# Soft-capped attention and two expert layers on one core: first loads in another order, fewer warming products, the first weight conversion at another place

## The chip, the cores and the metric

The kernel runs on one core of one Trainium2 chip. The time is the device time of one execution in microseconds; the median of three runs is given, and one more execution was taken by the hardware profiler.

## The reference

Three stages run in a row. The attention has 2 batches, 12 heads, 448 tokens and 64 columns a head; its scores are capped by a tanh. Two feed-forward layers follow on the 896 tokens with 768 columns. All is in 32-bit floats, except that the weights w_in, w_out of both layers come as 64-bit floats and are converted on the chip.

```python
scores = cap * np.tanh((q @ k.T / sqrt(64)) / cap)
attn = exp(scores - max(scores)); attn = attn / (sum(attn) + 1e-09)
x = (attn @ v)                                  # heads side by side: 896 x 768
h = x @ w_in                                    # 768 x 2048
x = (s * max(h, 0) ** 2 + b) @ w_out            # 2048 x 768
h = x @ w2_in                                   # 768 x 1024
so = h * softmax(h); ln = (so - mean) / sqrt(var + 1e-06) * g_ln
out = ln @ w2_out                               # 1024 x 768
```

## The kernel before, in words

**The start.** All that the first two pairs of heads need is loaded ahead of a branch. The keys go through load_by_key (line 98, its DMA is L104 when it is called by pair), the queries through load_by_query (line 119, its DMA is L123) or directly (L140). A DMA is issued by the engine whose queue is named: nc.sync is SyncE (SP in the profile), nc.scalar ScalarE (ACT), nc.gpsimd GpSimd (POOL). Each engine issues in its program's order. The scalar cap comes by L144; VectorE makes its absolute value a_t (L171), its reciprocal and the score factor sc_t from it, and each engine loads a_t (L183) and branches on it (L1006): up to 32 the arm layers(arm, False) runs, which is the case here (cap is 30). Meanwhile TensorE multiplies a tile of ones by itself 24 times (L170; in the profile each 32-bit product is two records), which gives no result that is used: the warming products.

**The attention.** The 24 heads are worked on as 12 pairs (0 to 11), four heads (two pairs) to a load group (0 to 5). For a pair, prep (line 401) turns keys and queries by products with an identity matrix (tiles pk, pq, L413), and splits each into a high and a low part: ScalarE makes the queries' high part (qh, L424), VectorE the rest. scores_by_key (line 441) makes four score tiles c = 0 to 3 of three product terms each on TensorE (s, L451), and ScalarE takes the tanh of each into e (L456). exps_by_key (line 459) has two exponentials on ScalarE (L463), two additions over the key blocks on GpSimd (c, L468 and L469) and two VectorE steps (L472). products_by_key (line 479) multiplies by the values (o, L484), and values_by_key (line 491) sums the rows by a product with ones (m, L498), and divides.

The loop over n runs from 0 to 13: it takes the scores of pair n, the exponentials of pair n - 1, the products of pair n - 2 and the prep of pair n + 2. on_pe keeps TensorE's instructions in the written order; tc.issue_after(x) queues the instructions of its block that run on x's engine behind x, and has no effect on other engines. The rest is placed by a scheduler. The next groups are loaded by load_group (line 379) when n is odd.

**The conversion.** The class Weights loads 64-bit weights into two buffers (raws, those that held the first keys and queries), 768 KB at a time from SyncE's queue (L281), and converts a block in steps: the first is an absolute value on ScalarE (L224), then VectorE steps (L225, L229, L234, L238), and a last step on both (L244, L245). weights.pump(1) takes one step in every turn of the loop from n = 3 on. It stands in `with tc.issue_after(st["dve"].ins)`, st["dve"] being VectorE's last instruction of values_by_key. weights.load(1) issues the loads of the first two blocks at n = 1.

**Behind the attention** both layers run as long rows of products on TensorE with the conversions beside them.

Of the kernel before, what the change touches and what calls it, by code (L numbers as in the profile page):

```python
# [37 lines left out]
def tile_softcap_attention__relu2__solu(  # L38
# [15 lines left out]
    nc = tc.nc  # L54
# [4 lines left out]
    P = 128  # L59
# [28 lines left out]
    cap_t = cst.tile([P, 1], F32, name="cap_t")  # L88
# [30 lines left out]
    def load_by_query(t, src, b, heads, eng=None):  # L119

        for pr in range((heads.stop - heads.start) // 2):
            for j in range(2):
                (eng or nc.sync).dma_start(  # L123
                    out=t[:, pr, :, j],
                    in_=src[b, heads.start + 2 * pr + j].rearrange("(p c) d -> p c d", c=NC),
                )

    first = {}
    for raw, nm, rows in ((raws[0], "k", P), (raws[1], "q", CP)):
        first[nm] = raw.bitcast(F32)[:rows, :4 * NC * D].rearrange(  # L130
            "p (n c h d) -> p n c h d", n=2, c=NC, h=2
        )
    for pr in range(2):
        pair = slice(2 * pr, 2 * pr + 2)
        odd = nc.scalar if pr == 0 else nc.sync
        for _ in load_by_key(first["k"][:, pr:pr + 1], k, 0, pair, by_pair=True, odd=odd):
            pass
        if pr == 0:
            for j, queue in enumerate((nc.sync, nc.scalar)):
                queue.dma_start(  # L140
                    out=first["q"][:, 0, :, j],
                    in_=q[0, j].rearrange("(p c) d -> p c d", c=NC),
                )
            nc.scalar.dma_start(out=cap_t, in_=cap.partition_broadcast(P))  # L144
        else:
            load_by_query(first["q"][:, 1:], q, 0, pair)
    ident = cst.tile([P, P], F32, name="ident")
    make_identity(nc, ident)
    s_t = cst.tile([P, 1], F32, name="s_t")
# [16 lines left out]

    with psum("ps_w", 1) as ps_w:
        idle = ps_w.tile([P, 512], F32, name="idle")
        for n in range(24):
            nc.tensor.matmul(idle[:D, :D], lhsT=ones, rhs=ones, start=True, stop=True)  # L170
    nc.vector.tensor_scalar(  # L171
        out=a_t.bitcast(U32), in0=cap_t.bitcast(U32), scalar1=0x7FFFFFFF, scalar2=None,
# [4 lines left out]
        out=sc_t, in0=r_t, scalar1=1.0 / float(D) ** 0.5, scalar2=None, op0=ALU.mult  # L177
# [7 lines left out]
    def layers(ctx, general):  # L185
# [191 lines left out]
        def load_group(g, names=("k", "q", "v")):  # L377
            b, i = divmod(g, GB)
            heads = slice(4 * i, 4 * i + 4)
            for nm, src in (("k", k), ("q", q), ("v", v)):  # L380
                if nm not in names:
                    continue
                by_key = nm != "q" and not general
                if g == 0 and (nm == "q" or nm == "k" and by_key):
                    nat[nm, g] = first[nm]
                    continue
                by_pair = nm != "v"
                shape = [P, 2, NC, 2, D] if by_pair else [P, 4, NC * D]
                t = ap_.tile(shape, F32, tag=f"{nm}n", name=f"{nm}n{g}", bufs=3)
                if by_key:  # L390
                    for _ in load_by_key(t, src, b, heads, by_pair):
                        pass
                elif by_pair:
                    t = t[:CP]
                    load_by_query(t, src, b, heads)
                else:
                    t = t[:CP]
                    nc.sync.dma_start(out=t, in_=by_query(src, b, heads))
                nat[nm, g] = t

        split = {}
        st = {}
# [41 lines left out]
        def scores_by_key(n, c):  # L444
            if c == 0:
                st["e", n] = ap_.tile([P, 7, S], F32, tag="e", name=f"e{n}", bufs=3)
            ps = ps_s.tile([P, 2, 512], F32, tag="s", name=f"s{n}_{c}")
            both = (slice(0, D), slice(D, P)) if c < 3 else (slice(0, P),)
            for x, (kk, qq) in enumerate(terms(n)):
                for j, rows in enumerate(both):  # L450
                    st["pe"] = nc.tensor.matmul(  # L451
                        ps[:, j, :S], lhsT=kk[rows, c * P:(c + 1) * P], rhs=qq[rows],
                        start=(x == 0), stop=(x == 2),
                    )
            m = len(both)
            nc.scalar.activation(  # L456
                out=st["e", n][:, 2 * c:2 * c + m, :], in_=ps[:, :m, :S], func=AF.Tanh
            )

# [214 lines left out]
        load_group(0, ("v",))  # L674
        load_group(2, ("k", "q"))
        load_group(1, ("v",))
        load_group(2, ("v",))
        NPR = NH // 2
        preps = {}

        def prep_half(n):
            if n < NPR:
                if n not in preps:
                    preps[n] = prep(n)
                next(preps[n], 0)

        if general:
            for n in range(NPR + 2):
                for c in range(NC):
                    i, c2 = 2 * n + c // 2, c % 2  # L690
                    if i < NH:
                        scores(i, c2)
                    if 0 <= i - 1 < NH:
                        exps(i - 1, c2)
                    if 0 <= i - 2 < NH:
                        transposes(i - 2, 2 * c2)
                        transposes(i - 2, 2 * c2 + 1)
                    if c < 2:
                        prep_half(n + 1)
                if n % 2 == 1 and n // 2 + 3 < NG:  # L700
                    load_group(n // 2 + 3)
                if n >= 2:
                    values(n - 2)
        else:
            def on_pe(step, *args):

                with tc.issue_after(st["pe"].ins):
                    step(*args)

            prep_half(1)  # L710
            prep_half(1)
            for n in range(NPR + 2):
                now, last = n < NPR, n >= 2
                for c in range(NC):
                    if now:
                        on_pe(scores_by_key, n, c)
                    if c == 1:
                        if 0 <= n - 1 < NPR:
                            exps_by_key(n - 1)
                        if last:  # L720
                            on_pe(products_by_key, n - 2, 0)
                if last:
                    on_pe(products_by_key, n - 2, 1)
                on_pe(prep_half, n + 2)
                on_pe(prep_half, n + 2)
                if last:
                    on_pe(values_by_key, n - 2)
                    with tc.issue_after(st["dve"].ins):
                        weights.pump((n > 2) if now else 3)
                if n == 1:  # L730
                    weights.load(1)
                if n % 2 == 1 and n // 2 + 3 < NG:
                    load_group(n // 2 + 3)
        att.close()
# [310 lines left out]
```

## Time and profile before

| | before |
|---|---|
| median of three runs | 484.4 us (482.73, 484.40, 484.58) |
| span of the profiled execution | 481.5 us; the page gives no other time of it |
| TensorE (PE) busy | 463.8 us, 96% |
| VectorE (DVE) busy | 352.2 us, 73% |
| ScalarE (ACT) busy | 275.8 us, 57% |
| GpSimd (POOL) busy | 88.6 us, 18% |
| mean granted TensorE clock | 0.989 |
| mean DMA rate | 102 GB/s |

The span runs from the first to the last instruction, and a run's time holds a little more. Busy time counts the instructions that work, not those that issue DMAs, branch or wait. A granted clock of 1.00 is 2.4 GHz, 0.50 is 1.2 GHz.

### The profile page before, as it was taken

Reading aid. Unit: us, or ns where it says so; the run is one execution under the profiler, and the core shown is the slowest. Engines: PE = TensorE matmul, PEld = TensorE weight load, DVE = VectorE, ACT = ScalarE, POOL = GpSimd, SP = SyncE. Lnnn points to the kernel's source line nnn. Section 1 sums busy time; section 2 is a strip of 40 time slices with the busy share of each in tenths; the row PEclk is TensorE's granted clock in tenths of the full one; section 3 lists DMA queues with packets and bytes.
Section 4 is the critical chain, followed back from the end, with each engine's and each line's share of the span. In section 5 each row is a group of like instructions: output and inputs, shape, how many; then the busy total and the mean of one; then the engine's idle time right before and its main releaser. Section 6 shows DMA issues by size and latency. Waiting matters only on the chain.

```text
span 481.5 us, 6595 instructions
## 1 busy us (share of the span) xinstructions
PE 463.8 (96%) x2432; PEld 376.6 (78%) x2432; DVE 352.2 (73%) x566; ACT 275.8 (57%) x398; POOL 88.6 (18%) x93
## 2 busy tenths in 40 slices
PE   7696999999999999999999999999999999999995
PEld 6443444444889989889988889989888898999894
DVE  3354999999898999996599988998958984043110
ACT  2877889982486577675577855555535552133120
POOL 4463879797000000000000000000001010000000
PEclk9898999999999999999999999999999999999998
DMA  4567533000456676642123324344312300011112
GB/s 96 126 177 170 121 96 103 1 1 0 154 175 195 210 230 207 181 159 83 50 87 89 93 88 139 124 136 165 131 66 67 131 1 13 21 33 34 34 45 61
DMA packets 47577, 49.28 MB, mean 102 GB/s; under 512 B 24496, under 2 KB 39984, under 8 KB 47536
## 3 DMA queue, kind: packets, MB, share of 16 engines
q1 hardware_dynamic: 46352, 48.54, 34.3%
q8 instruction: 21, 0.34, 0.3%
q10 hardware_dynamic: 1088, 0.23, 0.2%
q14 instruction: 20, 0.16, 0.1%
q0 software_dynamic: 96, 0.01, 0.0%
HBM read 46.01 MB, written 2.75 MB: 101 GB/s over the span
## 4 chain that ended last, share of the span: by engine, by line
PE 90%; SPq 5%; issue 2%; DMA 1%; ACTq 0%; ACT 0%; DVE 0%; DVEq 0%
PE in L329 8%; PE in L328 8%; PE y L330 8%; PE y L329 8%; PE y L328 8%; PE in L330 8%; PE o L484 7%; PE s L451 6%; PE h L919 4%; PE h L915 4%; PE h L923 4%; PE o L966 4%; PE o L965 4%; PE o L964 4%; SPq L104 2%; PE m L498 2%
## 5 line engine op out<-in xcount | busy, mean ns | idle before, releaser
L329 PE MATMUL in<-xl,h_wi 128*128 128x510 f32 (+2 forms) x192 | 70.0, 365 | 0.0
L328 PE MATMUL in<-xh,h_wi 128*128 128x510 f32 (+2 forms) x192 | 69.8, 365 | 0.0
L330 PE MATMUL in<-xh,l_wi 128*128 128x510 f32 (+2 forms) x192 | 69.6, 364 | 0.0
L900 POOL TENSOR_SCALAR va<-vs 128x1 f32<-128x1 f32 x7 | 2.0, 288 | 321.3 <-ACT e L899 321.3
L360 ACT ACTIVATE gh<-g,s_t 128x510 fp32r<-128x510 f32 (+1 forms) x64 | 42.2, 668 | 18.8 <-PE y L330 18.6
L361 DVE SCALAR_TENSOR_TENSOR gl<-g,s_t,gh 128x510 fp32r<-128x510 f32 (+1 forms) x64 | 42.7, 681 | 2.9 <-ACT gh L360 2.8
L484 PE MATMUL o<-e,vn 128*64 128x448 f32 x192 | 41.8, 561 | 0.0
L463 ACT ACTIVATE e<-e,a_t 128x1792 f32<-128x1792 f32 (+1 forms) x24 | 40.7, 1696 | 0.7
L456 ACT ACTIVATE e<-s 128x896 f32<-128x896 f32 (+1 forms) x48 | 36.6, 816 | 6.1 <-PE s L451 4.0
L329 PEld LDWEIGHTS in<-xl,h_wi 128*128 128x128 f32 x192 | 36.0, 188 | 5.0 <-issue 1.4
L328 PEld LDWEIGHTS in<-xh,h_wi 128*128 128x128 f32 x192 | 36.0, 188 | 4.3 <-issue 0.7
L330 PEld LDWEIGHTS in<-xh,l_wi 128*128 128x128 f32 x192 | 36.0, 188 | 3.6
L964 PE MATMUL o<-w2o_h,lh 128*128 128x384 f32 (+1 forms) x104 | 35.6, 342 | 0.5 <-ACT lh L206 0.5
L966 PE MATMUL o<-w2o_h,ll 128*128 128x384 f32 (+1 forms) x104 | 35.4, 342 | 0.0
L965 PE MATMUL o<-w2o_l,lh 128*128 128x384 f32 (+1 forms) x104 | 35.4, 340 | 0.0
L915 PE MATMUL h<-w2i_h,yh 128*128 128x512 f32 x84 | 33.0, 393 | 0.0
L919 PE MATMUL h<-w2i_l,yh 128*128 128x512 f32 x84 | 33.0, 392 | 0.0
L923 PE MATMUL h<-w2i_h,yl 128*128 128x512 f32 x84 | 32.8, 390 | 0.0
L472 DVE SCALAR_TENSOR_TENSOR c<-c,e 64x448 f32<-64x448 f32 x24 | 26.4, 1100 | 8.1 <-POOL c L469 7.7
L224 ACT ACTIVATE wt_wi<-raw 128x768 f32<-128x768 f32 x16 | 14.6, 911 | 27.7 <-DMA raw<-in_moe_w_in_dram 16.8
L451 PEld LDWEIGHTS s<-qh,kh 64*128 64x128 f32 (+1 forms) x84 | 9.3, 191 | 25.4 <-ACT e L456 17.4
L468 POOL TENSOR_TENSOR c<-e 128x896 f32<-128x896 f32 x12 | 25.3, 2111 | 20.0 <-ACT e L463 10.5
(422 smaller groups left out, 1110.1 us busy)
## 6 DMA issues: line engine op xcount, KB each, us to landing
raw<-in_moe_w_in_dram SPq DMA_DIRECT2D x16, 768.0 KB, 4.9
raw<-in_moe_w_out_dram SPq DMA_DIRECT2D x24, 512.0 KB, 3.6
raw_w2i<-in_moe_w_in_dram SPq DMA_DIRECT2D x12, 512.0 KB, 4.4
raw<-in_moe_w_out_dram SPq DMA_DIRECT2D x8, 768.0 KB, 4.4
qn<-in_q_dram SPq DMA_DIRECT2D x20, 112.0 KB, 3.0
vn<-in_v_dram SPq DMA_DIRECT2D x12, 128.0 KB, 3.2
kn<-in_k_dram SPq DMA_DIRECT2D x20, 64.0 KB, 2.5
vn<-in_v_dram SPq DMA_DIRECT2D x12, 96.0 KB, 3.0
```

The costliest lines, as they stand in the source:

```text
L328: nc.tensor.matmul(o, lhsT=wh, rhs=xh, start=first, stop=False)
L329: nc.tensor.matmul(o, lhsT=wh, rhs=xl, start=False, stop=False)
L330: nc.tensor.matmul(o, lhsT=wl, rhs=xh, start=False, stop=last)
L360: nc.scalar.mul(out=gh[:, :m], in_=r2, mul=s_t)
L361: nc.vector.scalar_tensor_tensor(out=gl[:, :m], in0=r2, scalar=s_t, in1=full(gh[:, :m]), op0=ALU.mult, op1=ALU.subtract,)
L484: st["pe"] = nc.tensor.matmul(o[j * D:(j + 1) * D, :S], lhsT=vn[:, 2 * (n % 2) + j, c * D:(c + 1) * D], rhs=st["e", n][:, 2 * c + j if c < ...
L915: nc.tensor.matmul(ps[:, n, :], lhsT=yh[:, kk, :], rhs=big["w2i_h"][:, kk, f], start=(kk == 0), stop=False,)
L919: nc.tensor.matmul(ps[:, n, :], lhsT=yh[:, kk, :], rhs=big["w2i_l"][:, kk, f], start=False, stop=False,)
L923: nc.tensor.matmul(ps[:, n, :], lhsT=yl[:, kk, :], rhs=big["w2i_h"][:, kk, f], start=False, stop=(kk == KD - 1),)
L964: nc.tensor.matmul(o, lhsT=lh[:, f, :], rhs=wh, start=(f == 0), stop=False)
L965: nc.tensor.matmul(o, lhsT=lh[:, f, :], rhs=wl, start=False, stop=False)
L966: nc.tensor.matmul(o, lhsT=ll[:, f, :], rhs=wh, start=False, stop=(f == KF2 - 1))
```

## The change

Cap is the first DMA on ScalarE's queue, and the queries of pair 1 are issued by GpSimd ahead of everything else that it does. The queries of load groups 1 and 2 go to GpSimd's queue too. There are 14 warming products in place of 24. The first two blocks of w_in are loaded ahead of the loop, before the values of group 2, which were loaded before them. The conversion's steps are also queued behind the last tanh that was written (ScalarE's), so that a step on ScalarE in turn n comes behind the fourth tanh of pair n.

```diff
+    nc.scalar.dma_start(out=cap_t, in_=cap.partition_broadcast(P))
+    load_by_query(first["q"][:, 1:], q, 0, slice(2, 4), nc.gpsimd)
     for pr in range(2):
...
-            nc.scalar.dma_start(out=cap_t, in_=cap.partition_broadcast(P))
-        else:
-            load_by_query(first["q"][:, 1:], q, 0, pair)
...
-        for n in range(24):
+        for n in range(14):
             nc.tensor.matmul(idle[:D, :D], lhsT=ones, rhs=ones, start=True, stop=True)
...
                 elif by_pair:
                     t = t[:CP]
-                    load_by_query(t, src, b, heads)
+                    load_by_query(t, src, b, heads, nc.gpsimd if g < 3 else None)
...
-            nc.scalar.activation(
+            st["act"] = nc.scalar.activation(
                 out=st["e", n][:, 2 * c:2 * c + m, :], in_=ps[:, :m, :S], func=AF.Tanh
             )
...
         load_group(2, ("k", "q"))
         load_group(1, ("v",))
-        load_group(2, ("v",))
...
             prep_half(1)
             prep_half(1)
+            weights.load(1)
+            load_group(2, ("v",))
             for n in range(NPR + 2):
...
-                    with tc.issue_after(st["dve"].ins):
+                    with tc.issue_after(st["dve"].ins), tc.issue_after(st["act"].ins):
                         weights.pump((n > 2) if now else 3)
-                if n == 1:
-                    weights.load(1)
```

ScalarE at the end of pair 2 and in pair 3, before (e is the tile of scores of a pair, s_0 to s_3 its four score tiles, qh the high part of the queries, wt_wi the conversion's tile, raw the weights as loaded):

```order
L456 ACTIVATE e_373<-s_3_410 128x448
L463 ACTIVATE e_373<-e_373,a_t 128x1344
L424 ACTIVATE qh_433<-pq_428,sc_t 128x448
L224 ACTIVATE wt_wi_531<-raw_58 128x768
L456 ACTIVATE e_452<-s_0_453 128x896
L456 ACTIVATE e_452<-s_1_461 128x896
L224 ACTIVATE wt_wi_1050<-raw_59 128x768
L463 ACTIVATE e_452<-e_452,a_t 128x1792
```

The same place after the change (lines are one less):

```order
L462 ACTIVATE e_363<-e_363,a_t 128x1344
L423 ACTIVATE qh_423<-pq_418,sc_t 128x448
L455 ACTIVATE e_442<-s_0_443 128x896
L455 ACTIVATE e_442<-s_1_451 128x896
L462 ACTIVATE e_442<-e_442,a_t 128x1792
L455 ACTIVATE e_442<-s_2_471 128x896
L455 ACTIVATE e_442<-s_3_479 128x448
L223 ACTIVATE wt_wi_521<-raw_58 128x768
L462 ACTIVATE e_442<-e_442,a_t 128x1344
```

The first step of the first conversion moved from ahead of pair 3's first tanh to behind its fourth, and that of the second conversion left pair 3; it now stands behind the fourth tanh of pair 9, and that of the third behind pair 11's.

SyncE's queue up to the first weights, before (kn, qn, vn are the tiles of keys, queries and values; 24 DMAs stand between the branch and the first row here):

```order
L123 DMA qn_208<-in_q_dram 112x4x64 x4
L109 DMA vn_213<-in_v_dram 64x2x256
L109 DMA vn_213<-in_v_dram 64x2x192
L109 DMA vn_213<-in_v_dram 64x2x256
L109 DMA vn_213<-in_v_dram 64x2x192
L109 DMA vn_220<-in_v_dram 64x2x256
L109 DMA vn_220<-in_v_dram 64x2x192
L109 DMA vn_220<-in_v_dram 64x2x256
L109 DMA vn_220<-in_v_dram 64x2x192
L281 DMA raw_58<-in_moe_w_in_dram 128x6x256
L281 DMA raw_59<-in_moe_w_in_dram 128x6x256
```

After the change (20 DMAs stand between the branch and the first row here):

```order
L109 DMA vn_203<-in_v_dram 64x2x256
L109 DMA vn_203<-in_v_dram 64x2x192
L109 DMA vn_203<-in_v_dram 64x2x256
L109 DMA vn_203<-in_v_dram 64x2x192
L280 DMA raw_58<-in_moe_w_in_dram 128x6x256
L280 DMA raw_59<-in_moe_w_in_dram 128x6x256
L109 DMA vn_230<-in_v_dram 64x2x256
L109 DMA vn_230<-in_v_dram 64x2x192
```

Of the 36 DMAs between the branch and the first weights eight queries left the queue and four values moved behind the weights, which leaves 24.

GpSimd from the branch on, after the change (before, the memsets stand there without the queries):

```order
L114 MEMSET kn_164 64x2x64 x2
L1039 ISA
L123 DMA qn_175<-in_q_dram 112x4x64
L1039 ISA
L123 DMA qn_175<-in_q_dram 112x4x64
L1039 ISA
L123 DMA qn_175<-in_q_dram 112x4x64
L1039 ISA
L123 DMA qn_175<-in_q_dram 112x4x64
L116 MEMSET vn_180 64x2x64 x2
L114 MEMSET kn_187 64x2x64 x2
```

The four queries of group 1 came in between the memsets; those of group 2 follow in the same way, before two more pairs of memsets, so that eight DMAs stand ahead of GpSimd's first addition. TensorE's order in this arm differs by the ten warming products alone.

## Rows read from the trace of the kernel before

**Rows 1.** The page, part 1: busy us, share of the span, instructions of TensorE.

```profile
PE 463.8 (96%) x2432; PEld 376.6 (78%) x2432; DVE 352.2 (73%) x566; ACT 275.8 (57%) x398; POOL 88.6 (18%) x93
```

**Rows 2.** Busy time by stretches: us, each engine's busy us, granted clock, DMA, GB/s.

```profile
14.00:17.00 3.00, 0.83 (x6) 0.66 (x7) 1.39 (x2) 2.08 (x3) 2.01 (x1) 0.99 0.60 135
17.00:20.40 3.40, 3.18 (x16) 2.12 (x14) 0.69 (x1) 2.72 (x3) 1.01 (x4) 0.51 0.71 182
...
41.00:44.30 3.30, 3.30 (x9) 1.51 (x11) 0.00 (x0) 3.04 (x3) 0.00 (x0) 0.51 0.33 74
46.90:109.60 62.70, 62.70 (x374) 30.54 (x376) 60.38 (x75) 55.23 (x57) 53.01 (x36) 1.00 0.26 64
```

**Rows 3.** Chain that ended last, 40 to 56 us: start us, us, what.

```profile
40.10 2.30 PE s L451 x9
...
46.86 1.42 PE s L451 x12
...
49.93 1.60 PE s L451 x9
...
55.06 1.43 PE s L451 x12
```

**Rows 4.** Timeline of TensorE: start, us, engine, line, out<-in, [idle before <-releaser].

```profile
1.01 5.38 PE L170 MATMUL idle<-ones 128*64 128x64 f32 x48 [1.01 <-DVE ones L163]
...
16.79 0.85 PE L413 MATMUL pq<-ident,qn 112*128 112x112 f32 x4 [1.60 <-DMA qn<-in_q_dram]
...
31.49 0.97 PE L498 MATMUL m<-c,ones 128*64 128x448 f32 x4
32.39 0.47 PE L451 MATMUL s<-qh,kh 64*128 64x448 f32 x2
...
40.10 0.47 PE L451 MATMUL s<-qh,kh 64*128 64x448 f32 x2 [4.55 <-ACT e L456]
```

**Rows 5.** Timeline of ScalarE, the same columns.

```profile
14.75 1.33 ACT L456 ACTIVATE e<-s 128x896 f32<-128x896 f32 x2
17.68 0.63 ACT L424 ACTIVATE qh<-pq,sc_t 128x448 fp32r<-128x448 f32 x1 [1.60 <-PE pq L413]
...
32.61 0.61 ACT L424 ACTIVATE qh<-pq,sc_t 128x448 fp32r<-128x448 f32 x1
38.34 0.89 ACT L224 ACTIVATE wt_wi<-raw 128x768 f32<-128x768 f32 x1 [5.12 <-POOL xh L521]
```

**Rows 6.** Timeline of the DMA issues of ScalarE (ACTq) and SyncE (SPq).

```profile
2.74 0.64 ACTq L144 DMA_DIRECT2D cap_t<-in_cap_dram  x1
...
8.16 5.13 SPq L104 DMA_DIRECT2D kn<-in_k_dram  x8
...
13.34 2.60 SPq L123 DMA_DIRECT2D qn<-in_q_dram  x4
...
32.05 1.09 SPq L281 DMA_DIRECT2D raw<-in_moe_w_in_dram  x2
```

**Rows 7.** DMA issues at 32.0, 4.9 to 5.5, 2.1: KB, us to landing.

```profile
raw<-in_moe_w_in_dram SPq DMA_DIRECT2D x1, 768.0 KB, 6.1
...
raw<-in_k_dram SPq DMA_DIRECT2D x1, 48.0 KB, 3.1
...
s_t<-in_moe_s_dram POOLq DMA_DIRECT2D x1, 0.5 KB, 3.2
```

**Rows 8.** Timeline of GpSimd, with its own DMA issues.

```profile
2.85 0.92 POOL L161 DMA_DIRECT2D g_t<-in_moe_g_ln_dram  x1
3.87 0.30 POOL masks.py:199 TENSOR_SCALAR_AFFINE_SELECT ident<-ident 128x128 f32<-128x128 f32 x1
7.39 0.45 POOL L114 MEMSET kn<- 64x128 f32 x2 [3.22 <-DVE sc_t L176]
...
14.99 2.08 POOL L468 TENSOR_TENSOR c<-e 128x896 f32<-128x896 f32 x1 [5.63 <-ACT e L463]
```

**Rows 9.** Timeline of VectorE: the two steps behind GpSimd's additions of pair 0.

```profile
21.99 1.27 DVE L472 SCALAR_TENSOR_TENSOR c<-c,e 64x448 f32<-64x448 f32 x2 [2.96 <-POOL c L469]
```

More of the change, by code (lines that the diff above doesn't have):

```diff
@@ L711, in layers @@
             prep_half(1)
+            weights.load(1)
+            load_group(2, ("v",))
             for n in range(NPR + 2):
```

## The prediction

> **What bounds the kernel now.** I read the page first: TensorE's busy share says that it is the limit over the whole [rows 1], so the question is where it isn't busy, and whether a shorter wait there reaches the end. A table by stretches answers the second half: from 46.9 to 109.6 us TensorE works 62.70 of 62.70 us at clock 1.00 [rows 2]. The chain shows the pairs of heads following each other there at a fixed step: the twelve products of one pair's first two score tiles begin at 46.86, those of the next at 55.06, 8.20 later [rows 3]. So a microsecond won before 46.86 is a microsecond at the end.
>
> Before that point TensorE is not the bound. Its timeline shows pair 3 beginning its scores at 32.39 and stopping: the second half starts at 40.10 after 4.55 us idle, released by ScalarE [rows 4]. ScalarE's own timeline says what held it: it ended the scaling of pair 4's queries at 33.2 (32.61 + 0.61) and next did not a tanh but L224, the first step of the conversion of the expert weights, at 38.34 [rows 5]. L224 stands in front of pair 3's tanh in ScalarE's order and needs a block of w_in that SyncE's queue issues at 32.05 [rows 6] and that lands 6.1 us later [rows 7], at 38.15. (The row names POOL as its releaser, but that instruction does not write what L224 reads; the landing fits to 0.2 us.) So what bounds up to 39 us is the SyncE queue, issue after issue from 8.16 to 32.05.
>
> **The change, part by part.** The sum is made on the profiled execution, whose span is 481.5 us. The median of the three runs is 484.4, 2.9 us above; I carry that difference over unchanged.
>
> *The conversion behind the pair's last tanh, and the weights sooner.* These two remove the same stall and are counted once. Without it pair 4 would start one step after pair 3, at 32.39 + 8.20 = 40.59; it starts at 46.86, so the stall costs 6.27 us. Of that, 4.55 is idle time and 1.72 what the low clock behind it cost: the second half of pair 3's scores took 2.30 us against 1.60 a pair later [rows 3], and the products with the values behind it ran slow too, at a granted clock of 0.51, the 1.2 GHz level [rows 2]. Either edit would do alone. For the weights: two DMAs of pair 1's queries leave SyncE ahead of the group loads, at some 0.65 each (eight issues take 5.13 [rows 6]), so the first of those goes out at 8.16 - 1.3 = 6.9. Then 24 issues stand ahead of w_in where 36 did in 23.9 us: 6.9 + 24 x 0.66 = 22.8, landed at 28.9. L224, behind pair 3's fourth tanh, comes after the pair's second score half, which ends 4.7 us after its first begins (49.93 + 1.60 against 46.86 [rows 3]): not before 35. What is late next? ScalarE is busy 55.23 of 62.70 us in the even stretch [rows 2], 7.2 of a step of 8.20; with L224 (0.89) 8.1, just under it. VectorE is busy 60.38 there and gets no work. The conversions are pumped per pair, not by time, so the stage behind the attention finds its weights as ready as now. **Term: -6.25.**
>
> *Queries of groups 1 and 2 on GpSimd's queue.* Pair 1's scores stand behind the transposes of pair 2, whose queries SyncE issues from 13.34 on [rows 6]. TensorE waited 1.60 us for them at 16.79 [rows 4]; ScalarE, with four tanh done at 16.08, stood still until 17.68 [rows 5]. Issued from GpSimd at about 8 us they land near 12, and the keys 1.3 sooner than now, so ScalarE goes straight on to an exponential. All of that gap is on the path, as ScalarE is the bound from there to pair 3. **Term: -1.6.** A rule of the notes speaks against this edit. The Trainium skill ("DMA: Bandwidth & Descriptors", section "Issuing engines are not separate DMA queues") says that transfers issued by several engines run on the same 16 DMA engines, and that spreading them saves issue time alone, usually small beside the transfer. By it this term would be near 0 and the sum 484.4 - 6.25 = 478.15. The row differs: four issues take 2.60 us and twelve stand ahead, so it is issuing that these queries wait for.
>
> GpSimd pays for it. A small transfer that it issues holds it for 0.92 us [rows 8]; no row shows one of 112 KB. I take 0.92, the only row of the same kind, with 0 below and 2.08 above (the longest GpSimd instruction at hand [rows 8]). From 7.39 us it does a memset pair (0.45), eight such DMAs (7.36) and four memset pairs (1.8), so its first addition for pair 0 starts at 17.0 instead of 14.99. Who waits is TensorE, for pair 0's row sums, at 31.49 now [rows 4] and 29.9 in my forecast. Between lie that addition (2.08), a memset pair (0.45), the second addition (2.08) and two VectorE steps (1.27 [rows 9]), so it may start as late as 29.9 - 5.88 = 24.0. The eight DMAs may then take 24.0 - 7.39 - 0.45 - 1.8 = 14.4 us, 1.8 each: term 0. At 2.08 each the cost would be 8 x 0.28 = 2.2.
>
> *Cap first, two queries of pair 1 on GpSimd.* Cap's issue moves from 2.74 to 0.73, ScalarE's first place [rows 6], so the branch on it can come up to 2.0 us sooner. But TensorE has pair 1's transposes ahead of the first scores, and pair 1's keys keep their places on SyncE: the last, issued at 4.9 to 5.5, lands 3.1 later [rows 7], at 8.0 to 8.6, about when those transposes run now. The identity matrix, ready on GpSimd at 4.2 [rows 8], comes 1.8 later, at 6.0, under the same cover. Bounds -2.0 to 0; I take 0, to which the keys' row is nearest.
>
> *Fourteen warming products.* 24 take 5.38 us from 1.01 on [rows 4]; 14 take 3.14 and end at 4.15, when nothing of pair 0 could be transposed anyway. Term 0 as work; as a clock risk it is a rival.
>
> **Sum:** -6.25 - 1.6 = -7.85. The span becomes 473.65 and the time **476.55**.
>
> **The rivals.**
> *A, the clock falls early.* With warming done at 4.15 TensorE stands for longer until the first keys. Rows 2 show what sparse work does: after 0.83 busy us in 3.0 the granted clock was 0.51 for 3.4 us. Should that come at the first scores, it costs at most half of 3.4, 1.7 us (1.72 in pair 3): 478.25. Against it: TensorE's products there are few, and ScalarE takes over as the bound soon.
>
> *B, the conversion's new place costs.* In three pairs an L224 of 0.89 now stands ahead of an exponential. If TensorE waits for it each time, 2.7 comes back: 479.25. For it: 8.1 is hardly under 8.20. Against it: a conversion step is in that busy time already.
>
> *C, slower, as GpSimd becomes the bound.* If a 112 KB issue holds GpSimd for as long as its smallest transfer takes to land, 3.2 us [rows 7], instead of 0.92, the additions come late: 476.55 + 8 x (3.2 - 1.8) = 487.75. It decides from 1.8 us per DMA, and the whole gain is gone at 1.8 + 7.85 / 8 = 2.78. Against it: the 0.92. A rule of the Trainium skill ("SBUF — State Buffer", section "SBUF: two separate sides") speaks for it: GpSimd cannot write its descriptors while VectorE is in certain fast modes, and 0.62 us became 3.1 in its example. By that rule the time is that of C; VectorE was idle beside the row of this trace, which therefore decides nothing on it.
>
> *D, the change doesn't act:* the stall stays and only the 1.6 goes, 482.8. The changed order, with L224 behind the fourth tanh, speaks against it.
>
> **How the numbers follow.** A measurement of this kernel tells some 0.5% (2.4 us) from no change. Chances: the forecast 0.50, A 0.27, B 0.12, C 0.05, D 0.03, GpSimd late by less (1.8 to 2.78 per DMA, 476.55 to 484.4) 0.03. The forecast, A and B are faster by over 0.5% (under 482.0), and so is about half of the last: 0.90. The other half, D and a part of C make "same": 0.06. Slower: 0.04. The range goes down by the 2.0 of cap's bound to 474.5 and up to A and B together, 476.55 + 1.7 + 2.7 = 480.95, so 481.0.
>
> **What would show it.** Right: no idle time before pair 3's second half, and pair 4 starting near 39.0; w_in issued near 23; no gap before the scaling of pair 2's queries; steps of 8.2 us as before. Wrong: a GpSimd DMA of over 1.8 us with TensorE waiting for the row sums; a granted clock of 0.5 while the first scores run; TensorE waiting for ScalarE in the pairs with an L224.

## The result and the profile after

| | before | after |
|---|---|---|
| median | 484.21 us (4 runs, 482.73 to 484.58) | 477.19 us (4 runs, 476.14 to 478.09) |
| ratio | 1 | 0.9864, 95% interval 0.984 to 0.9887 |
| profiled execution: time, span | not given, 481.5 us | 478.09 us, 476.3 us |

The change is faster by 7.0 us, 1.4%. The forecast was 476.55, 0.64 too low, and the time lies in the range. Two of its steps were wrong all the same, as the experiments show. The execution profiled after the change is the slowest of its four runs: their spans are 474.2, 475.1, 475.7 and 476.3.

The page, part 1, after the change:

```profile
PE 463.2 (97%) x2412; PEld 376.9 (79%) x2412; DVE 351.8 (74%) x566; ACT 275.9 (58%) x398; POOL 95.6 (20%) x103
```

Against [rows 1] the work is the same but for TensorE's ten warming products less and GpSimd's ten query DMAs more. (A DMA that GpSimd issues does count among its busy time, 7.0 us for these ten, unlike what the note under the table of the kernel before says.) So what went is waiting.

The chain that ended last, of the kernel after (start us, us, what):

```profile
4.79 4.16 DMA raw<-in_k_dram
...
20.29 2.91 PE s L450 x9
24.79 2.15 PE s L450 x10
...
33.74 1.43 PE s L450 x12
...
41.96 1.43 PE s L450 x12
...
50.18 1.43 PE s L450 x12
```

Against [rows 3]: pair 3 begins at 33.74 and pair 4 one even step of 8.22 later; the stall is gone and the step is what it was. New is that the chain runs over TensorE at 20.29 and 24.79, in pairs 1 and 2, with score products that take 2.91 where such nine take 1.60 later [rows 3].

The timeline of TensorE after the change (start us, us, engine, line, what, idle before and its releaser):

```profile
1.01 3.25 PE L169 MATMUL idle<-ones 128*64 128x64 f32 x28 [1.01 <-DVE ones L162]
6.31 1.09 PE L412 MATMUL pk<-ident,raw 128*128 128x128 f32 x4 [2.05 <-POOL ident masks.py:199]
...
11.50 0.57 PE L450 MATMUL s<-ql,kh 64*128 64x448 f32 x2
...
20.29 0.74 PE L450 MATMUL s<-qh,kh 64*128 64x448 f32 x2 [1.81 <-ACT e L455]
...
33.67 0.48 PE L450 MATMUL s<-qh,kh 64*128 64x448 f32 x2
...
36.76 0.47 PE L450 MATMUL s<-qh,kh 64*128 64x448 f32 x2
```

The last row answers to the 4.55 us of idle time in [rows 4]: pair 3's second half has no wait. Pair 3's first half, though, begins at 33.67, 1.28 later than the 32.39 of [rows 4].

The timeline of ScalarE:

```profile
12.49 1.73 ACT L455 ACTIVATE e<-s 128x896 f32<-128x896 f32 x2 [0.79 <-PE s L450]
...
18.82 0.61 ACT L423 ACTIVATE qh<-pq,sc_t 128x448 fp32r<-128x448 f32 x1
19.33 1.71 ACT L455 ACTIVATE e<-s 128x896 f32<-128x896 f32 x2
...
24.83 0.63 ACT L423 ACTIVATE qh<-pq,sc_t 128x448 fp32r<-128x448 f32 x1 [0.64 <-PE pq L412]
...
34.65 1.73 ACT L455 ACTIVATE e<-s 128x896 f32<-128x896 f32 x2 [0.97 <-issue]
...
39.41 0.93 ACT L223 ACTIVATE wt_wi<-raw 128x768 f32<-128x768 f32 x1
```

The conversion's first step stands at 39.41 and waits for nothing; in [rows 5] it waited 5.12. The 1.60 before pair 2's query scaling [rows 5] is gone (18.82). Two waits are new, 0.64 before pair 3's query scaling and 0.97 before pair 3's first tanh.

Busy time by stretches, columns as in [rows 2]; then, from the timelines, the issues of SyncE (SPq) and GpSimd, GpSimd's first addition, and VectorE's wait for b:

```profile
20.40:26.40 6.00, 6.00 (x27) 4.74 (x29) 3.30 (x5) 5.32 (x6) 3.22 (x4) 0.50 0.62 172
46.90:109.60 62.70, 62.70 (x369) 29.78 (x366) 60.47 (x74) 52.43 (x54) 52.66 (x36) 1.00 0.20 52
```

```profile
6.30 5.53 SPq L104 DMA_DIRECT2D kn<-in_k_dram  x8
22.94 1.10 SPq L280 DMA_DIRECT2D raw<-in_moe_w_in_dram  x2
7.09 2.86 POOL L123 DMA_DIRECT2D qn<-in_q_dram  x4 [0.31 <-issue]
16.28 2.10 POOL L467 TENSOR_TENSOR c<-e 128x896 f32<-128x896 f32 x1 [1.58 <-ACT e L462]
8.71 0.24 DVE L742 CAST gh<-b_t 128x2 fp32r<-128x2 f32 x2 [4.81 <-DMA b_t<-in_moe_b_dram]
```

The first weights are issued at 22.94 (forecast 22.8), and four query DMAs hold GpSimd for 2.86, 0.72 each. At 1.2 GHz TensorE is busy 6.00 of 6.00 us from 20.4 to 26.4: it is the bound there, as the chain says.

**Where the time went.** From the first tanh to pair 1's first it is 19.33 - 12.49 = 6.84 us, where before it was 8.41 (11.20 and 19.61 in ScalarE's timeline there): 1.57 won, the forecast's 1.6. From there to pair 3's first scores it is 33.67 - 19.33 = 14.34, where it was 32.39 - 19.61 = 12.78: 1.56 given back. ScalarE's two new waits, 0.64 + 0.97, are as long (the second lies just behind that point: from pair 1's first tanh to pair 3's it is 34.65 - 19.33 = 15.32 here and 13.76 in run e2 below, which has neither wait). And the first tanh is 1.29 late: pair 1's keys are transposed at 9.19, where it was 8.74, as they landed 4.16 after their issue in place of the 3.1 of [rows 7], and from the first transposes to the first scores TensorE runs at half rate (the score row of 0.57 above takes 0.36 in pair 1). So pair 4 starts at 41.96 where the forecast had 39.0, and the profiled span is 476.3 in place of 473.65.

### The profile page after: what moved, and what is told of

The parts are those of the page before. It is cut to its first block, busy times and chain, and to the rows that moved or that the text cites. A ratio compares the mean times of both kernels' runs of the same rounds, so it can differ in the third digit from the quotient of the medians.

```text
span 476.3 us, 6578 instructions
## 1 busy us (share of the span) xinstructions
PE 463.2 (97%) x2412; PEld 376.9 (79%) x2412; DVE 351.8 (74%) x566; ACT 275.9 (58%) x398; POOL 95.6 (20%) x103
## 4 chain that ended last, share of the span: by engine, by line
PE 95%; ACT 2%; DMA 2%; DVE 0%; SPq 0%; issue 0%
PE in L328 8%; PE o L483 8%; PE in L327 8%; PE y L329 8%; PE y L328 8%; PE y L327 8%; PE in L329 8%; PE s L450 7%; PE h L914 4%; PE h L918 4%; PE h L922 4%; PE o L964 4%; PE o L965 4%; PE o L963 4%; PE m L497 2%; DMA raw<-in_k_dram 2%
## 5 line engine op out<-in xcount | busy, mean ns | idle before, releaser
L205 ACT CAST lh<-x 128x512 fp32r<-128x512 f32 x14 | 7.5, 590 | 35.7 <-PE o L964 35.6
L223 ACT ACTIVATE wt_wi<-raw 128x768 f32<-128x768 f32 x16 | 14.6, 912 | 22.7 <-DMA raw<-in_moe_w_in_dram 12.7
```

## The experiments

Two theories are set against each other. The prediction's: the stall is worth 6.25, either of two edits removes it, and queries on GpSimd are worth another 1.6. The rival: nearly all of the gain is one edit, and the others cost or win nothing that the end sees. Times are medians, each with the kernel before on the same chip; ratios are to that.

**The conversion's place alone, e2** (on the kernel before):

```diff
-            nc.scalar.activation(
+            st["act"] = nc.scalar.activation(
...
-                    with tc.issue_after(st["dve"].ins):
+                    with tc.issue_after(st["dve"].ins), tc.issue_after(st["act"].ins):
```

> The kernel before with one edit alone: the conversion's steps queued behind the pair's last tanh. Theory: this edit alone removes the stall in pair 3 (6.25 us): 478.0 us, pair 4 starting near 40.6 instead of 46.86, although w_in still lands at 38. Rival: w_in is still late, L224 now holds the exponential behind it until 38 and TensorE waits for that instead: 480 to 483.

Measured: 476.69 (476.63 to 476.9, 5 runs) beside 483.3; 0.9861 [0.9833, 0.9888]. That is 6.6 us, all that the whole change wins (0.9864), and 1.3 below what was expected. Its ScalarE (timeline) and its chain:

```profile
33.30 1.73 ACT L456 ACTIVATE e<-s 128x896 f32<-128x896 f32 x2
...
38.25 0.93 ACT L224 ACTIVATE wt_wi<-raw 128x768 f32<-128x768 f32 x1
```

```profile
40.62 1.43 PE s L451 x12
```

Pair 3's tanh no longer waits, and pair 4 starts at 40.62, where the prediction's term has 40.59. The weights still go out at 32.18, as late as before; the step behind the fourth tanh takes them up as they come.

**The weights sooner alone, e3** (on the kernel before):

```diff
+            weights.load(1)
+            load_group(2, ("v",))
             for n in range(NPR + 2):
...
-                if n == 1:
-                    weights.load(1)
```

(The load of group 2's values ahead of it is taken out, as in the change.)

> The kernel before with one edit alone: the first two blocks of w_in loaded ahead of group 2's values. The prediction said that either edit alone would do. The built order puts the first L224 behind pair 2's fourth tanh and a second one in front of pair 3's first tanh. If the prediction holds: 478. Theory now: w_in goes out only four issues (2.6 us) sooner, lands near 35.5 and its second block near 38, so pair 3's tanh still waits for it and nothing is won: 483.5 to 485.

Measured: 484.0 (482.62 to 484.72, 12 runs), 1.0013 [0.9997, 1.0029]: nothing won. Its ScalarE and, last, its TensorE (timelines):

```profile
34.73 0.90 ACT L224 ACTIVATE wt_wi<-raw 128x768 f32<-128x768 f32 x1 [3.79 <-POOL c L468]
35.53 1.49 ACT L463 ACTIVATE e<-e,a_t 128x1344 f32<-128x1344 f32 x1
36.93 0.62 ACT L424 ACTIVATE qh<-pq,sc_t 128x448 fp32r<-128x448 f32 x1
37.95 0.90 ACT L224 ACTIVATE wt_wi<-raw 128x768 f32<-128x768 f32 x1 [0.40 <-DMA raw<-in_moe_w_in_dram]
38.75 1.72 ACT L456 ACTIVATE e<-s 128x896 f32<-128x896 f32 x2
```

```profile
39.71 0.57 PE L451 MATMUL s<-qh,kh 64*128 64x448 f32 x2 [4.40 <-ACT e L456]
```

The weights were issued at 29.35 and the step ran at 34.73, 3.6 sooner than in [rows 5]. But in ScalarE's order it also stands further forward: ahead of pair 2's last exponential and of pair 4's query scaling, which it stood behind in [rows 5]. What it held up before it holds up still, with an exponential and a scaling more, and the second conversion's step stands ahead of pair 3's tanh as well. TensorE waits 4.40 in place of 4.55. The run came out as expected of it, not as the prediction had it.

**Queries of groups 1 and 2 on GpSimd: alone (e4), with the conversion's place (e10), and taken out of the change (e7).** The line, which e7 puts back:

```diff
-                    load_by_query(t, src, b, heads)
+                    load_by_query(t, src, b, heads, nc.gpsimd if g < 3 else None)
```

> The kernel before with one edit alone: the queries of groups 1 and 2 on GpSimd's queue. Theory: the gap of 1.6 us before pair 2's query scaling goes, and w_in goes out eight issues sooner, at about 26.8, landing near 33 beside the tanh that waits for it, so most of the stall goes too: 477.5 to 480. Rival: the queue's place of w_in does not matter as the scheduler pulls L224 forward: only the 1.6 us, 482.6.

> The kernel before with two edits: the conversion behind the last tanh, and the queries of groups 1 and 2 on GpSimd's queue; cap, pair 1's queries, the warming and w_in's place as before. Theory: the sum of the prediction without any of the edits at the start, -6.25 and -1.6: 475.3 to 475.6 against the 476.7 of the conversion alone. Rival: the 1.6 is not on the path, as TensorE at the low clock takes over as the bound in pairs 1 and 2: 476.3 to 477.

> The changed kernel with the queries of groups 1 and 2 back on SyncE's queue. Theory: the gap of 1.6 us before pair 2's query scaling comes back in part, as SyncE starts 1.3 us sooner than before and the low clock has moved the first tanh later: 477.5 to 478.7 us. Rival: the queries on GpSimd win nothing because their eight transfers slow the keys beside them: 476.5 to 477.3.

| | time (runs) | ratio |
|---|---|---|
| e4, before + queries | 481.38 (12) | 0.9961 [0.9944, 0.9978] |
| e10, e2 + queries | 476.65 (6) | 0.9861 [0.9839, 0.9883] |
| e7, after - queries | 477.26 (6) | 0.9878 [0.9855, 0.99] |

With the conversion in its new place no gain from the queries' queue is seen: e10 has e2's ratio, 0.9861. This pair alone could hide some 1.7 us. But the change beside e7 (0.0014 lower) and e11 beside e12 further down (0.0001 higher) are the same edit in two more kernels, and the three together make a gain of 0.2 us, uncertain by 1.0. e10 and e7 came out as their rivals had it. Alone (e4) the edit wins 1.9 us, which neither expectation had. It is near the 1.6, but the rows say by another way: with eight DMAs off SyncE's queue the weights are issued at 26.96, and ScalarE's two conversion steps, now further forward still, end the stall sooner (e4, timeline of ScalarE; pair 3's first tanh is the last row, 39.14 in the kernel before):

```profile
32.83 0.90 ACT L224 ACTIVATE wt_wi<-raw 128x768 f32<-128x768 f32 x1 [3.66 <-DMA raw<-in_moe_w_in_dram]
33.63 1.33 ACT L456 ACTIVATE e<-s 128x896 f32<-128x896 f32 x2
35.29 0.90 ACT L224 ACTIVATE wt_wi<-raw 128x768 f32<-128x768 f32 x1 [0.33 <-DMA raw<-in_moe_w_in_dram]
...
38.01 1.72 ACT L456 ACTIVATE e<-s 128x896 f32<-128x896 f32 x2
```

By the chains pair 4 begins 2.39 sooner than before. Of that 0.77 is the earlier second half of pair 3 (39.33 against 40.10), and the rest that its products run at 2.4 GHz there: 1.61 and 1.65 us in place of 2.30 and 2.59 (granted clock 1.00 from 39.4 to 42.5; 0.51 in [rows 2]).

**Warming products: 14 alone (e5, on the kernel before), 24 in the changed kernel (e1).** The line of e5, which e1 turns round:

```diff
-        for n in range(24):
+        for n in range(14):
```

> The kernel before with 14 warming products instead of 24, nothing else. Theory: the first transposes and scores run at half rate in every execution and the first tanh comes some 1.3 us later; ScalarE is the bound from there to the stall, and w_in lands at 38 whatever TensorE does, so the wait in pair 3 swallows most of it: within 0.5 us of before in time (483.3), the products slow in the profile. Rival: the rate does not depend on the ten products; then the four key transposes take 0.63 us and the first tanh stays at 11.2 us.

> The change with 24 warming products instead of 14, all else as changed. Theory: in the changed kernel the first transposes and scores run at half rate (four key transposes 1.09 us instead of 0.63, score products 0.375 us apart instead of 0.205), because the shorter warming does not bring TensorE to the full rate; with 24 the first transposes take 0.63 again, the first tanh comes near 11.3 us instead of 12.49, and pair 4 starts 1 to 3 us sooner than 41.96: 474.5 to 476.2 us. Rival: what delays the first scores is the landing of pair 1's keys (4.16 us after issue), beside the queries that GpSimd now loads; then the products turn fast, the first tanh moves by less than 0.5 us, and the time stays within 0.5 us of the changed kernel's 477.2.

Measured: e5 483.86 (483.07 to 485.41, 12 runs), 1.0016 [1.0001, 1.0031]; e1 476.62 (475.8 to 476.8, 5 runs), 0.9859 [0.9831, 0.9887]. So the kernel before loses 0 to 1.5 us with fourteen, but e5's rows don't put that at the start: pair 1's first tanh comes at 19.07 there (19.61 before), and what is longer is the slow stretch behind the stall, 2.90 and 3.19 us for the 2.30 and 2.59 of before. In the changed kernel nothing can be told between 14 and 24 (0.9864, 0.9859): e1 missed its expected time by 0.4 us, though its one profile starts pair 4 at 39.73, 2.2 sooner than the profile after. In two of the three profiles with 14 (after, e5) the first transposes of keys run at half rate, in the third (e7) those behind them; in e1, as in the kernel before, they don't (timelines of TensorE: e5, then e1). With 24 they do in some profiles too, of which more at the end.

```profile
1.01 3.25 PE L170 MATMUL idle<-ones 128*64 128x64 f32 x28 [1.01 <-DVE ones L163]
7.61 1.09 PE L413 MATMUL pk<-ident,raw 128*128 128x128 f32 x4 [3.35 <-DMA raw<-in_k_dram]
```

```profile
1.01 5.37 PE L169 MATMUL idle<-ones 128*64 128x64 f32 x48 [1.01 <-DVE ones L162]
6.31 0.66 PE L412 MATMUL pk<-ident,raw 128*128 128x128 f32 x4
```

**The first loads: alone (e6, on the kernel before), with identity and b ahead of the queries (e8), with pair 1's keys on two queues (e9).** e6 takes the change's first four lines alone. e8 is the changed kernel with 24 warming products and with the identity matrix and b's load ahead of these queries (their old places, not shown, are taken out):

```diff
     nc.scalar.dma_start(out=cap_t, in_=cap.partition_broadcast(P))
+    ident = cst.tile([P, P], F32, name="ident")
+    make_identity(nc, ident)
+    b_t = cst.tile([P, 1], F32, name="b_t")
+    nc.gpsimd.dma_start(out=b_t, in_=b_in.partition_broadcast(P))
     load_by_query(first["q"][:, 1:], q, 0, slice(2, 4), nc.gpsimd)
```

e9 adds to e8

```diff
-        odd = nc.scalar if pr == 0 else nc.sync
+        odd = nc.scalar
```

> The kernel before with two edits of the change alone: cap goes out first on ScalarE's queue, and pair 1's queries of group 0 go out on GpSimd ahead of its small loads. 24 warming products, and the conversion at its old place. Theory (the prediction's term of 0 between -2.0 and 0): the first tanh is set by the first keys, the identity and the warmed TensorE, not by cap or by pair 1's queries, so the time stays at that of the kernel before (within 0.5 us of it), the wait of about 4.5 us before pair 3's second half stands, and VectorE waits for b's load behind the queries on GpSimd. Rival: pair 1's keys and queries were what pair 1's start waited for; then the first tanh of pair 1 to 3 come about 1 us sooner and the time is 1 to 2 us lower. Second rival: VectorE's wait for b holds kh and kl of pair 0 and the time is 0.5 to 1 us higher.

> The changed kernel with 24 warming products, and with the identity matrix and b's load ahead of the queries on GpSimd. Theory: in the changed kernel VectorE stands 4.8 us for b, whose load GpSimd now issues behind two transfers of queries, with the first splitting of keys queued behind it; with b first that wait ends before 5 us, the scores no longer wait 0.72 us for the query's low part as they do with 24 products alone, and pair 4 starts 0.7 to 1.0 us sooner than there (39.73): 475.6 to 476.0. Rival: the landing of pair 1's keys near 8.6 us bounds, nothing moves: 476.4 to 476.8.

> The changed kernel with 24 warming products, with the identity and b's load ahead of the queries on GpSimd, and with half of pair 1's keys on ScalarE's queue instead of all on SyncE's. Theory: pair 1's keys then land at about 7.5 to 8.5 us in place of 9.3, but pairs 0 to 2 are set by ScalarE, so pair 3's first tanh stays within 0.7 us of 32.3 and the time is 476 to 477, as with the identity first. Rival: the issue on ScalarE (about 0.65 us each) stands ahead of the first tanh and costs as much as it takes, 477 to 478. Second rival: the wait for pair 1's keys (1.49 us before its transposes) was on the path, 475 to 475.8.

| | time (runs) | ratio |
|---|---|---|
| e6 | 485.2 (11) | 1.004 [1.0025, 1.0054] |
| e8 | 476.97 (6) | 0.9877 [0.9848, 0.9905] |
| e9 | 477.97 (6) | 0.9886 [0.9863, 0.991] |

e6 missed all its expectations: it is 1.9 us slower by the ratio. Up to pair 2 little is lost by it (its first tanh comes at 26.50, at 26.28 in the kernel before). The loss comes behind that, and begins again at the place of the conversion (ScalarE's timeline in e6; the third row is the second conversion's step, and pair 3's first tanh comes at 39.77):

```profile
35.79 0.93 ACT L223 ACTIVATE wt_wi<-raw 128x768 f32<-128x768 f32 x1 [2.88 <-POOL c L467]
36.62 0.61 ACT L423 ACTIVATE qh<-pq,sc_t 128x448 fp32r<-128x448 f32 x1
38.96 0.91 ACT L223 ACTIVATE wt_wi<-raw 128x768 f32<-128x768 f32 x1 [1.73 <-DMA kn<-in_k_dram]
```

Pair 4's query scaling, at 32.61 in [rows 5], now stands behind the step. By the chains pair 4 begins 1.73 later than before: the second half of pair 3 starts 0.62 later (40.72), and its products, slow for longer, take 2.90 and 3.09 us in place of 2.30 and 2.59. So e6 doesn't price the first loads by themselves; the stall with the slow stretch behind it grows or shrinks by about 2 us (e4, e6) where the conversion's steps have moved in ScalarE's order. e8 takes away VectorE's 4.81 us wait for b (1.14 there, over at 5.00), and the time doesn't fall; it lies above both its expectations. So no run shows that this wait was on the path. e9's second half of keys, issued on ScalarE from 3.61 on, came no sooner (TensorE waits 1.69 for them, where it was 1.49 in e8); its time is in its first rival's stretch, but can't be told from e8's by the ratios.

**Is it the clock? e11 and e12.** Both are the changed kernel with 24 warming products and idle products that keep TensorE busy in pairs 0 and 1; e12 also has the queries of groups 1 and 2 back on SyncE.

```diff
+            for _ in range({(0, 3): 6, (1, 1): 14}.get((n, c), 0)):
+                st["pe"] = nc.tensor.matmul(
+                    ps[:D, 1, S:S + D], lhsT=ones, rhs=ones, start=True, stop=True,
+                )
             st["act"] = nc.scalar.activation(
```

> The changed kernel with 24 warming products, and with 20 idle products of the warming's kind (64 rows of output, 64 columns of ones) added: 6 behind pair 0's last scores, 14 behind pair 1's second scores, written beside the scores where nothing reads. Theory: TensorE's low clock at about 20 to 23 us comes because it has little to do while ScalarE sets the pace (1.8 us idle before it); filled, that stretch keeps the full clock, the six transposes and scores there go back from 0.57 to 1.05 us to 0.37 to 0.66 us, ScalarE has no idle time before pair 3's first tanh, and pair 3 starts 0.3 to 1 us sooner than 32.4, with the time 475.6 to 476.5. Rival: the low clock in that stretch is not what ScalarE waits for (it had 0.25 us idle there with 24 products), so the time stays at 476.6 although the clock reads 1.00. Second rival: the idle products stand ahead of scores that ScalarE wants and the time is 0.5 to 2 us higher.

> The kernel with 24 warming products and 20 idle products of the last call, with the queries of groups 1 and 2 back on SyncE's queue; TensorE should have the full clock from the first score to pair 4 here as there, so that what the queries' queue is worth is not mixed with the clock. Theory (the prediction's term of 1.6, eaten by the clock in the changed kernel): queries land at about 17 again, ScalarE has 1 to 1.6 us idle before pair 2's query scaling, pair 3's first tanh comes at 33.2 to 33.9 in place of 32.27, and the ratio to the kernel before is 0.989 to 0.990 where 0.9867 was measured with the queries on GpSimd. Rival: the time does not see that gap at all; the ratio stays at 0.9867 within 0.001 even if the gap is in the trace, or the queries land early enough from SyncE and there is no gap.

Measured: e11 476.19 (476.11 to 477.61, 5 runs), 0.9867 [0.9844, 0.9889]; e12 476.8 (476.03 to 477.5, 6 runs), 0.9866 [0.984, 0.9892]. The mechanism is there (by stretches, e1 and then e11; below them e11's timelines, TensorE and ScalarE):

```profile
21.00:22.00 1.00, 1.00 (x5) 0.81 (x5) 0.44 (x1) 1.00 (x2) 0.00 (x0) 0.50 0.61 149
```

```profile
21.00:22.00 1.00, 0.99 (x9) 0.77 (x7) 0.85 (x2) 1.00 (x1) 0.23 (x2) 1.00 0.36 70
```

```profile
17.43 1.85 PE L456 MATMUL s<-ones 128*64 128x64 f32 x28
19.31 0.47 PE L450 MATMUL s<-qh,kh 64*128 64x448 f32 x2
...
32.27 1.73 ACT L459 ACTIVATE e<-s 128x896 f32<-128x896 f32 x2
```

With the idle time ahead of pair 1's second half filled (1.81 us after the change), the clock stays at 2.4 GHz, and ScalarE runs to pair 3 without a wait. But pair 3's first tanh comes only 0.15 sooner than in e1 (32.42), less than the 0.3 to 1 expected, and the time is that of e1 within what can be told. e12 fell on its rival's side, and for a plain reason (SyncE, ScalarE):

```profile
11.46 2.60 SPq L123 DMA_DIRECT2D qn<-in_q_dram  x4
...
18.41 0.61 ACT L423 ACTIVATE qh<-pq,sc_t 128x448 fp32r<-128x448 f32 x1
```

With pair 1's queries off SyncE, group 1's are issued at 11.46 from SyncE too, in place of 13.34 [rows 6], and there is no gap left for GpSimd to close. e6, with its scaling at 18.56 straight behind an exponential, shows the same, and so does e7, the change without the queries' edit (timeline of ScalarE):

```profile
18.98 0.61 ACT L423 ACTIVATE qh<-pq,sc_t 128x448 fp32r<-128x448 f32 x1
```

No kernel here beats e2 or the changed kernel by more than can be told: the medians without the stall lie between 476.19 and 477.97.

## Why the prediction was right, and where it was wrong

**-6.25 for the stall: right.** e2 measures 6.6 for the conversion's place alone, and its profiled span, 475.0, is the 481.5 - 6.25 = 475.25 of this term; its pair 4 starts at 40.62, forecast 40.59.

**"Either edit would do alone": wrong.** e3 wins nothing. The step took the load's time as 22.8, which it is only with the queries' edits beside it (22.94 after, 28.04 in e7, 29.35 in e3), and it took ScalarE's order as fixed. In each of the kernels without the conversion edit (before, e3, e4, e5, e6) ScalarE meets the step ahead of pair 3's tanh and stands there for 2.88 to 5.12 us; where in the order it stands moved with every edit of the loads. That a schedule made for an earlier load puts the step earlier is how I read it; the rows show the place, not the scheduler's reason. No run has the load at 22.9 with the step in its old place, so whether so early a load would have done stays open.

**-1.6 for the queries: the gap was real, its worth in time was not found.** In the profile after the change 1.57 us are won there and 1.56 given back before pair 3. The prediction weighed the clock (rival A) at the first scores, and priced the queries as if the stretch behind the gap would keep its length. What I left out: with the gap gone TensorE is still the idle engine in pair 1, since ScalarE sets the pace; behind its 1.81 us of idle time the granted clock is 0.50, and from 20.4 to 26.4 it is TensorE that ScalarE waits for. And the late start hides the gap in the other kernel: in e2 the first tanh comes at 12.48, so of the 1.60 before pair 2's scaling 0.25 is left, and the pairs go on from the queries' landing whatever the start was. The profiles, one execution each, in order of span (first tanh of pairs 0, 1 and 3, from the timelines of ScalarE):

| | pair 0 | pair 1 | pair 3 | span |
|---|---|---|---|---|
| e1, 24 warming | 11.47 | 18.32 | 32.42 | 474.0 |
| e8, identity first | 11.18 | 18.02 | 32.27 | 474.1 |
| e11, filled | 11.52 | 18.36 | 32.27 | 474.3 |
| e2, conversion alone | 12.48 | 19.54 | 33.30 | 475.0 |
| e10, e2 + queries | 11.95 | 18.64 | 32.93 | 475.1 |
| e12, filled, no queries | 11.79 | 18.93 | 33.17 | 475.2 |
| e7, after - queries | 12.34 | 19.50 | 33.62 | 475.5 |
| after | 12.49 | 19.33 | 34.65 | 476.3 |
| e9, keys on two queues | 12.62 | 19.66 | 35.10 | 476.6 |

Without the gap a good start wins up to 1.0 on e2 (474.0 against 475.0), and a slow one loses as much or more (476.3, 476.6). That fits the scatter, 476.63 to 476.9 in five runs of e2 and 475.35 to 478.82 in six of e8; that it is the cause was not tried apart. Nor is all of a span settled by pair 3's first tanh: from there to the end these profiles take 441.5 to 442.2. On the medians nothing of the 1.6 is seen. (Landing "near 12" doesn't follow from the prediction's own rows either: the fourth DMA would start at 10.6 and land 3.2 later, near 13.8. The queries are wanted later than that, so nothing hangs on it.) The prediction also gave the gap to the wrong edit: pair 1's queries off SyncE close it alone (e7, e12).

The Trainium skill ("DMA: Bandwidth & Descriptors", section "Issuing engines are not separate DMA queues") would have put this term near 0, and the times agree as far as they can tell (e10 beside e2). Its reason does not fit the rows: issuing was what the queries waited for, since a place nearer the front of SyncE's own queue (e12) brought them in time as well.

**Cap and pair 1's queries, 0 within -2.0 to 0: not settled.** e6 gives +1.9 in a kernel whose stall it reshapes; in the changed kernel no run took these edits out by themselves. Nearest come e1 and e10, which differ by these edits and by the weights' place in SyncE's queue: 0.9859 and 0.9861, so nothing is seen, within some 1.7 us. **Fourteen products, 0: not settled either,** 0 to 1.5 in a kernel whose stall comes between (e5). **GpSimd, 0: right,** 0.70 to 0.72 per DMA of groups 1 and 2, under the 0.92 taken and far from 1.8; its first addition starts at 16.28 (forecast 17.0) and no engine waits longer for it. No run here shows what the Trainium skill's rule on GpSimd's descriptors ("SBUF — State Buffer", section "SBUF: two separate sides") says: GpSimd's issues of 112 KB took no longer while VectorE worked (0.70 each from 10.90 on, with VectorE busy for 1.97 of 2.00 us) than while it stood still (0.82 each from 1.32 on), and whether it was then in one of the modes meant, no row tells.

**The rivals.** A came true in part: the clock fell, but in pairs 1 and 2, at some 1.6 us, near the 1.7 worked out; and the first scores, where A looked for it, ran at half rate by their durations (0.57), which is part of the late start, though the granted clock reads 1.00 there. B did not: pair 4 follows one step of 8.22 behind pair 3, with L223 in between, and TensorE's timeline has no wait in the two later pairs with an L223 either. C and D did not. Of the marks named, "pair 4 near 39.0" failed (41.96): 1.29 of the 2.96 is the start, 1.56 the clock. The median came out only 0.64 above the forecast for two reasons that offset this: the profiled execution is 0.9 above its kernel's median, and the 2.9 carried over from the span of before was too much: after the change 478.09 stands beside a span of 476.3, so some 1.8 belong around a span, and the other 1.1 were that the median lay above the profiled execution. That the forecast came so near is luck.

## What to carry to other kernels

An instruction that waits for a load belongs behind the work that others wait for, in the order of its engine; starting the load sooner did not do the same here, where the instruction moved forward with it. A gap that is closed ahead of a stretch pays only if that stretch can take it up: ask which engine is idle there, what clock it will have behind the idle time, and whether another edit of the same change closes the gap already. And price an edit in the kernel in which it will stand: the same line was worth 1.9 us in one kernel (e4) and no gain that could be measured in another (e10).

## What the runs showed that was not expected

TensorE's first products ran at one of two rates in kernels in which TensorE's program is the same up to there, and the record of the clock doesn't always show it. With 24 warming products in each, the warming took 5.37 us in e1, 4.80 in e11 and 4.43 in e12, and the first scores ran at full rate in the first two and, but for the first of them, at half in the third. In the kernel after, the stretch in which a transpose of keys took 1.09 us stands in the table at 1.00; in e5, with the same 1.09, at 0.50 (after, then e5):

```profile
8.00:10.00 2.00, 1.58 (x8) 1.26 (x8) 1.26 (x6) 0.64 (x1) 1.96 (x4) 1.00 0.74 162
```

```profile
8.00:10.00 2.00, 2.00 (x12) 2.00 (x11) 1.24 (x3) 0.47 (x1) 0.99 (x5) 0.50 0.45 102
```

So the durations of like instructions tell a slow stretch where the granted clock doesn't. And a small load that stands behind large ones in GpSimd's order is late: b, issued at 4.36, let VectorE go on at 8.71, and where it went out first, at 1.28, at 5.00 (e8), though here the end didn't see it. It is the later issue that makes it late: it landed 4.2 us behind it in the one and 3.6 in the other.
